# Unpacking 64-bit weights in a fused attention and feed-forward kernel: signs by GpSimd, half of a rescaling by ScalarE, one VectorE operation per block, scales from sums of squares

## The chip, the cores and the metric

The kernel runs on one core of one Trainium2 chip. The metric is the device time of one execution in microseconds (us), the median over runs. A profile of one execution is at hand: it lists every instruction with its engine, its start and its length, and what released it from a wait. PE is the matrix engine (TensorE), PEld its weight loads, DVE is VectorE, ACT is ScalarE, POOL is GpSimd, SPq is the queue on SyncE that issues the DMAs.

## The reference

Linear attention with exponential features, then a feed-forward layer with two weight matrices. Attention has 8 batches, 8 heads, 576 positions and head size 64; the feed-forward layer sees 4608 tokens of width 512 and has a hidden width of 2048.

```python
def phi(x):
    proj = np.einsum('bhsd,df->bhsf', x, w_phi)
    proj = proj - np.max(np.abs(proj), axis=-1, keepdims=True)
    return np.concatenate([np.exp(proj), np.exp(-proj)], axis=-1)
q_p, k_p = (phi(q), phi(k))
kv = np.einsum('bhsf,bhsd->bhfd', k_p, v)
z = np.sum(k_p, axis=2)
num = np.einsum('bhsf,bhfd->bhsd', q_p, kv)
den = np.einsum('bhsf,bhf->bhs', q_p, z)[..., None] + 1e-06
attn = num / den
...
h = x @ w_in          # x: attn as [4608, 512]
g = h * (1.0 / (1.0 + np.exp(-1.702 * h)))
return (g @ w_out).astype(np.float32)
```

The two weight matrices w_in [512, 2048] and w_out [2048, 512] arrive as 64-bit floats. The chip has no 64-bit arithmetic, so the kernel takes each number apart as two 32-bit words, `hi` (sign, exponent, upper bits of the mantissa) and `lo`.

## The kernel before, in words

Everything is recorded first: each operation on an engine goes into a list with its tiles and a group (`part`) with a due time. A planner (`Recorder.schedule`) then simulates the engines with estimated costs and writes out one fixed order per engine. Every engine, and the DMA queue on SyncE, later works through its own list strictly in that order. All planned instructions therefore carry line 346, the line that emits them, and are told apart by their tiles. Pools of tiles marked as ordered are handed out in the order of recording.

Attention runs batch by batch in four units of two heads; the first six units take a path with 32-bit products (`project_whole`: transposes with `ident`, products with `wb`, tiles `ab` for batch 0). Each unit ends with quotients `xf` (a reciprocal `rc`, a product), transposes of `xf` by PE, and two copies into the tile `x`, which the feed-forward layer reads. The last 64 positions of a batch go through `zt` (`attn_last`). The feed-forward layer (`moe_chunk`) works on 256 or 384 columns of `x` at a time: products with the first weights into `hb`, tanh (`th`), `g`, its split into two 16-bit parts `gh` and `gl`, products with the second weights into `ab`. The first two chunks run in two parts of the hidden width, so that they can start when half of the weights is there; the first part's result is kept (`kept`, written into an `x` tile).

The weights are 32 blocks of 128 x 512: block i is one of w_in for even i, of w_out for odd i, j = i // 2. `wbuf` holds one 32-bit block each in 33 slots. A block arrives as 512 KB of 64-bit numbers, either in a free stretch at the end of `wbuf` (12 blocks) or in one of three `x` tiles (20 blocks, two to a tile); the other users of the three `x` tiles are the batches' attention outputs. `load_weights` then unpacks it:

- POOL writes `y` = hi times 2^-112 into the block's slot, as a float (the 64-bit exponent moved into 32-bit range);
- ACT turns `lo` into its upper three bits, in place;
- DVE shifts y left by 3 and ORs the bits of lo in (`x<-wbuf,x`, or `wbuf<-wbuf`), then a second DVE operation takes the sign bit from hi and ORs it in, which gives the number in its slot (`wbuf<-x`, or `wbuf<-wbuf`);
- PE sums |number| over the partitions with the constant `pick`, in four products with 128 columns, on the 16 upper bits of the number without sign, which lie in the staging tile. So PE is the last reader of the staging tile.

After 16 blocks `weight_scales` makes a power of two from the largest sum, per matrix, with a short chain between DVE and PE; after it `split_weights` writes each block as two 16-bit parts (one ACT and one DVE operation per block, `wbuf<-wbuf,sw`). Only then can the feed-forward products of that half begin.

Of the kernel before, what the change touches and what calls it, by code (L numbers as in the profile page):

```python
# [8 lines left out]
F32 = mybir.dt.float32  # L9
F32R = mybir.dt.float32r  # L10
F16 = mybir.dt.float16
BF16 = mybir.dt.bfloat16
I32 = mybir.dt.int32
U32 = mybir.dt.uint32
# [335 lines left out]
def attn_moe_kernel(ctx, tc, q, k, v, w_phi, w_in, w_out, out):  # L350
# [76 lines left out]
    ones = cp.tile([16, P], F32, name="ones")  # L427
    nc.gpsimd.memset(ones, 1.0)

# [39 lines left out]

    NS = NJ // NH + 1  # L470
    pick = cp.tile([P, 2 * NS - 1], BF16, name="pick")
    nc.gpsimd.memset(pick, 0.0)
    nc.gpsimd.memset(pick[:, NS - 1 : NS], 1.0)

    def load_weights(j, wsum, first, last):
# [4 lines left out]
        for i, src in (  # L480
# [4 lines left out]
            if not WIDE:  # L485
# [3 lines left out]
                z = new("osb")  # L489
                R.scalar.activation(z, wbuf[:, i + 1], AF.Abs)  # L490
            else:
# [3 lines left out]
                else:  # L495
# [4 lines left out]
                lo, hi = r32[:, :, 0], r32[:, :, 1]  # L500
                y = wbuf[:, i + 1]
                R.gpsimd.tensor_scalar(y, hi.bitcast(F32), 2.0**-112, None, ALU.mult)
                z = lo
                R.scalar.activation(z, lo.bitcast(U32), AF.Copy, scale=0.9375 * 2.0**-29)
                R.vector.scalar_tensor_tensor(
                    z, y.bitcast(I32), 3, z, ALU.logical_shift_left, ALU.bitwise_or
                )
                R.vector.scalar_tensor_tensor(
                    dst.bitcast(I32), hi, -(2**31), z, ALU.bitwise_and, ALU.bitwise_or
                )  # L510
                z = raw.bitcast(BF16).rearrange("p (n w) -> p n w", w=4)[:, :, 1]

            r = NS - 1 if i % 2 else j % (NS - 1)
            for c in range(NCT):
                R.tensor.matmul(
                    wsum,
                    pick[:, NS - 1 - r : 2 * NS - 1 - r],
                    z[:, c * P : (c + 1) * P],
                    start=first and i % 2 + c == 0,
                    stop=last and i % 2 == 1 and c == NCT - 1,  # L520
                    skip_group_check=True,
                )
# [22 lines left out]
    def weight_scales(k, wsum):  # L545

        m = small(1, "sc")[0:NS]
        m2 = small(NS, "sc")[0:NS]
        R.vector.tensor_reduce(m, wsum, AX.X, ALU.max)
        pow2(m, m)  # L550
        R.vector.tensor_scalar(m2, ident[0:NS, 0:NS], m, None, ALU.mult)
        tp = psa()
        R.tensor.matmul(tp[:, 0:NS], ones[0:NS], m2, start=True, stop=True)
# [693 lines left out]
```

## Time and profile before

| | |
|---|---|
| median of 3 runs | 1096.73 us (1096.34 to 1098.07) |
| the profiled execution | 1097.82 us, span in the profile 1096.0 us, mean granted clock of PE 0.993 |
| PE busy | 1062.2 us (97%) |
| DVE busy | 857.8 us (78%) |
| ACT busy | 712.2 us (65%) |
| POOL busy | 242.4 us (22%) |

Busy time is that of whole instructions. The end of a matrix product is modelled in the profile, so a busy PE can hold some waiting. In rows of groups of instructions the columns are engine, operation, output and input tiles, shapes and types, count, then either least, median and largest length in ns with the first and last start in us, or busy time in us and mean length in ns followed by the engine's idle time in front of them and what ended it. In rows in order of time the first number is the start in us from the span's start, the second the length in us, and a bracket tells the idle time before it and its releaser.

### The profile page before, as it was taken

To read this page: it belongs to the slowest core of one execution; us is meant where nothing else is said; L and a number is where in the kernel's file an instruction comes from. 1 tells how busy PE (TensorE), PEld (TensorE's weight loads), DVE (VectorE), ACT (ScalarE), POOL (GpSimd) and SP (SyncE) were. 2 spreads that over 40 slices of the span, in tenths; PEclk is the share of its full clock that TensorE was granted. 3 is DMA by queue.
4 is the path that set the end of the run, shared out by engine and by line. 5 is a ranking of instruction groups with operands and counts; after the bars stand their busy time and mean duration, and the time that the engine had idled before them with its cause. 6 is when DMAs were issued, how large, how long until landed. Compare 5 with 4: busy or idle time off the path is not lost.

```text
span 1096.0 us, 22834 instructions
## 1 busy us (share of the span) xinstructions
PE 1062.2 (97%) x8915; PEld 733.2 (67%) x8915; DVE 857.8 (78%) x1775; ACT 712.2 (65%) x1483; POOL 242.4 (22%) x310
## 2 busy tenths in 40 slices
PE   5997999999999999999999999999999999999997
PEld 3664677778766666678766666677876666577653
DVE  5889988999989997897789987897779877422322
ACT  4576687977677776676777677685677666432423
POOL 6546201322121212221132221121123111100000
PEclk9998999999999999999999999999999999999999
DMA  8854233454243431442243433333223220000101
GB/s 273 277 185 130 76 92 84 79 107 98 61 93 92 96 89 36 81 107 57 32 102 88 109 88 55 64 97 60 49 68 68 39 59 10 11 30 1 30 1 29
DMA packets 174252, 87.80 MB, mean 80 GB/s; under 512 B 140224, under 2 KB 164928, under 8 KB 173888
## 3 DMA queue, kind: packets, MB, share of 16 engines
q1 hardware_dynamic: 174144, 86.34, 33.0%
q8 instruction: 70, 1.15, 0.5%
q14 instruction: 38, 0.31, 0.1%
HBM read 54.59 MB, written 9.44 MB: 58 GB/s over the span
## 4 chain that ended last, share of the span: by engine, by line
PE 78%; DVE 10%; ACT 4%; issue 3%; DMA 2%; POOL 1%; SPq 1%; ACTq 0%; DVEq 0%; POOLq 0%
PE ab L346 31%; PE hb L346 29%; PE at L346 19%; DMA xT<-xs 1%; DVE sm L346 1%; DVE gl L346 1%; ACT e L346 1%; DVE ks L346 1%; DVE g L346 1%; DVE t L346 1%; ACT eh L346 1%; SPq L346 1%; DVE el L346 1%; DVE elb L346 1%; DMA tl<-in_v_dram 1%
## 5 line engine op out<-in xcount | busy, mean ns | idle before, releaser
L346 PE MATMUL hb<-x,wbuf 128*128 128x192 f16 (+3 forms) x3264 | 474.9, 280 | 1.1 <-DVE g L346 1.1
L346 PE MATMUL ab<-wbuf,gh 128*128 128x512 f16 x1152 | 335.8, 380 | 0.8 <-ACT gh L346 0.6
L346 PEld LDWEIGHTS <-wbuf 128*128 128x128 f16 x3264 | 279.1, 98 | 78.0 <-issue 0.9
L346 ACT ACTIVATE th<-hb,usc 128x384 f32<-128x384 f32 (+1 forms) x208 | 116.4, 560 | 130.7 <-PE hb L346 125.0
L346 PE MATMUL ab<-wbuf,gl 128*128 128x512 f16 x576 | 192.2, 380 | 1.3 <-DVE gl L346 1.1
L346 DVE SCALAR_TENSOR_TENSOR g<-th,hb 128x384 f32<-128x384 f32 (+1 forms) x208 | 107.6, 517 | 89.8 <-ACT th L346 87.5
L346 PEld LDWEIGHTS <-gh 128*128 128x128 f16 x1152 | 107.3, 98 | 80.4 <-ACT gh L346 2.9
L346 ACT ACTIVATE gh<-g,al 128x384 f16<-128x384 f32 (+1 forms) x176 | 107.6, 611 | 62.7 <-DVE g L346 62.4
L346 DVE SCALAR_TENSOR_TENSOR gl<-g,al,gh 128x384 f16<-128x384 f32 (+1 forms) x176 | 110.9, 630 | 39.2 <-ACT gh L346 32.9
L346 POOL TENSOR_TENSOR xf<-nf,rc 128x512 f32<-128x512 f32 x28 | 32.8, 1171 | 459.4 <-DVE rc L346 395.1
L346 PE MATMUL at<-ph,xT 128*128 128x128 f16 x944 | 108.6, 221 | 0.4 <-ACT x L346 0.4
L346 ACT ACTIVATE e<-at 128x512 f32<-128x512 f32 x144 | 85.6, 602 | 30.3 <-PE at L346 28.5
L346 DVE TENSOR_REDUCE sm<-at 128x4 f32<-128x512 f32 x126 | 86.1, 683 | 21.3 <-PE at L346 21.1
L346 ACT ACTIVATE e<-t 128x512 f32<-128x512 f32 x144 | 89.9, 640 | 9.8 <-DVE t L346 8.6
L346 PEld LDWEIGHTS <-gl 128*128 128x128 f16 x576 | 55.1, 98 | 51.1 <-DVE gl L346 7.2
L346 DVE SCALAR_TENSOR_TENSOR t<-at,ks,sm 128x512 f32<-128x512 f32 x118 | 87.5, 744 | 1.0
L346 DVE TENSOR_TENSOR el<-e,eh 128x512 f16<-128x512 f32 (+1 forms) x106 | 74.7, 704 | 12.7 <-ACT eh L346 11.1
L346 PE MATMUL at<-vs,eh 128*128 128x132 f32 x208 | 80.2, 386 | 0.0
L346 DVE TENSOR_TENSOR elb<-e,eh 128x512 bf16<-128x512 f32 x104 | 74.8, 719 | 6.7 <-ACT eh L346 6.5
L346 PEld LDWEIGHTS <-xT 128*128 128x128 f16 x944 | 70.2, 98 | 14.3 <-issue 1.3
L346 PE MATMUL at<-kzs,eh 128*128 128x132 f32 x216 | 78.2, 375 | 0.0
L346 ACT ACTIVATE eh<-t 128x512 fp32r<-128x512 f32 x105 | 66.4, 648 | 0.3 <-DVE t L346 0.2
(205 smaller groups left out, 1896.4 us busy)
## 6 DMA issues: line engine op xcount, KB each, us to landing
vn<-in_v_dram SPq DMA_DIRECT2D x64, 128.0 KB, 2.9
kq<-in_k_dram SPq DMA_DIRECT2D x32, 256.0 KB, 3.2
kq<-in_q_dram SPq DMA_DIRECT2D x32, 256.0 KB, 3.0
tl<-in_v_dram SPq DMA_DIRECT2D x18, 384.0 KB, 3.2
x<-in_moe_w_in_dram SPq DMA_DIRECT2D x10, 512.0 KB, 5.3
x<-in_moe_w_out_dram SPq DMA_DIRECT2D x10, 512.0 KB, 4.8
out_dram<-osb SPq DMA_DIRECT2D x38, 128.0 KB, 2.4
out_dram<-osb SPq DMA_DIRECT2D x16, 256.0 KB, 2.5
```

The source lines that it names most:

```text
L346: f(*[g(a) for a in o.args], **{k: g(a) for k, a in o.kw.items()})
```

## The change

Four things change for each block. POOL no longer writes y for even blocks: ACT does (an activation with a scale), POOL still does for odd blocks. POOL gets a new operation for every block: it compares hi with zero and multiplies the outcome by -32768, written as a 16-bit integer into the upper half of each word of `lo` (so after ACT has written lo). DVE keeps one operation out of two: y shifted left by 3, OR lo, which now has the sign in it, in place in y. And PE squares the block: each 128 x 128 piece is multiplied with itself (its own columns as weights and as moving data, 16 upper bits of the finished number in its slot), added up per matrix in a 128 x 256 tile `wsq`, whose largest element is the largest sum of squares. `weight_scales` reduces the 128 partitions of wsq on DVE, transposes the result by PE, reduces again, halves the exponent with integer operations, and goes on as before. The constant `pick` and its two memsets go; a small constant `wone` comes.

```diff
--- before.py
+++ after.py
@@ -11,6 +11,7 @@
 F16 = mybir.dt.float16
 BF16 = mybir.dt.bfloat16
 I32 = mybir.dt.int32
+I16 = mybir.dt.int16
 U32 = mybir.dt.uint32
 I64 = mybir.dt.int64
 AF = mybir.ActivationFunctionType
@@ -424,8 +425,11 @@
     nc.vector.tensor_copy(ii[0:D], ident[0:D, 0:D])
     nc.vector.tensor_copy(ii[D:P], ident[D:P, D:P])
 
-    ones = cp.tile([16, P], F32, name="ones")
+    ones = cp.tile([2, P], F32, name="ones")
     nc.gpsimd.memset(ones, 1.0)
+    wone = cp.tile([2, 2], F32, name="wone")
+    nc.vector.tensor_scalar(wone[:, 0:1], ident[0:2, 0:1], 16.0, None, ALU.mult)
+    nc.vector.tensor_copy(wone[:, 1:2], ident[0:2, 1:2])
 
     wst = static("wst", [P, NF], F32)
     wb = static("wb", [P, 2 * NF], F32)
@@ -466,13 +470,7 @@
         )
         R.vector.tensor_scalar(dst, dst, 2.0**-50, None, ALU.max)
 
-
-    NS = NJ // NH + 1
-    pick = cp.tile([P, 2 * NS - 1], BF16, name="pick")
-    nc.gpsimd.memset(pick, 0.0)
-    nc.gpsimd.memset(pick[:, NS - 1 : NS], 1.0)
-
-    def load_weights(j, wsum, first, last):
+    def load_weights(j, wsq, first, last):
         js = slice(j * P, (j + 1) * P)
         stage = None
         if WIDE and (j % 4 > 1 or j >= NJ - 4):
@@ -486,8 +484,6 @@
                 if i % 2 == 0:
                     dst = dst.rearrange("p (c f) -> p c f", c=NCT)
                 R.sync.dma_start(dst, src)
-                z = new("osb")
-                R.scalar.activation(z, wbuf[:, i + 1], AF.Abs)
             else:
                 if stage is None:
                     s0 = NBLK - 7 + 2 * (i % 4)
@@ -498,24 +494,28 @@
                 R.sync.dma_start(rd, src)
                 r32 = raw.bitcast(I32).rearrange("p (n w) -> p n w", w=2)
                 lo, hi = r32[:, :, 0], r32[:, :, 1]
+
                 y = wbuf[:, i + 1]
-                R.gpsimd.tensor_scalar(y, hi.bitcast(F32), 2.0**-112, None, ALU.mult)
-                z = lo
-                R.scalar.activation(z, lo.bitcast(U32), AF.Copy, scale=0.9375 * 2.0**-29)
-                R.vector.scalar_tensor_tensor(
-                    z, y.bitcast(I32), 3, z, ALU.logical_shift_left, ALU.bitwise_or
+                R.scalar.activation(lo, lo.bitcast(U32), AF.Copy, scale=0.9375 * 2.0**-29)
+                if i % 2:
+                    R.gpsimd.tensor_scalar(y, hi.bitcast(F32), 2.0**-112, None, ALU.mult)
+                else:
+                    R.scalar.activation(y, hi.bitcast(F32), AF.Copy, scale=2.0**-112)
+                sign = raw.bitcast(I16).rearrange("p (n w) -> p n w", w=4)[:, :, 1]
+                R.gpsimd.tensor_scalar(
+                    sign, hi.bitcast(F32), 0.0, -(2.0**15), ALU.is_lt, ALU.mult
                 )
                 R.vector.scalar_tensor_tensor(
-                    dst.bitcast(I32), hi, -(2**31), z, ALU.bitwise_and, ALU.bitwise_or
+                    y.bitcast(I32), y.bitcast(I32), 3, lo, ALU.logical_shift_left, ALU.bitwise_or
                 )
-                z = raw.bitcast(BF16).rearrange("p (n w) -> p n w", w=4)[:, :, 1]
-
-            r = NS - 1 if i % 2 else j % (NS - 1)
+
+            z = wbuf[:, i + 1].bitcast(BF16).rearrange("p (n w) -> p n w", w=2)[:, :, 1]
             for c in range(NCT):
+                zc = z[:, c * P : (c + 1) * P]
                 R.tensor.matmul(
-                    wsum,
-                    pick[:, NS - 1 - r : 2 * NS - 1 - r],
-                    z[:, c * P : (c + 1) * P],
+                    wsq[:, i % 2],
+                    zc,
+                    zc,
                     start=first and i % 2 + c == 0,
                     stop=last and i % 2 == 1 and c == NCT - 1,
                     skip_group_check=True,
@@ -542,17 +542,25 @@
         R.tensor.matmul(tp[:, P : P + 1], ones[0:1], m2, start=True, stop=True)
         R.vector.tensor_copy(dst, tp[:, P : P + 1])
 
-    def weight_scales(k, wsum):
-
-        m = small(1, "sc")[0:NS]
-        m2 = small(NS, "sc")[0:NS]
-        R.vector.tensor_reduce(m, wsum, AX.X, ALU.max)
-        pow2(m, m)
-        R.vector.tensor_scalar(m2, ident[0:NS, 0:NS], m, None, ALU.mult)
+    def weight_scales(k, wsq):
+
+
+
+        m = small(2, "sc")
+        m1 = small(1, "sc")[0:2]
+        m2 = small(2, "sc")[0:2]
+        R.vector.tensor_reduce(m, wsq, AX.X, ALU.max)
         tp = psa()
-        R.tensor.matmul(tp[:, 0:NS], ones[0:NS], m2, start=True, stop=True)
-        R.vector.tensor_reduce(wg[:, k, 0:1], tp[:, 0 : NS - 1], AX.X, ALU.max)
-        R.vector.tensor_copy(wg[:, k, 1:2], tp[:, NS - 1 : NS])
+        R.tensor.transpose(tp[0:2, 0:P], m, ident)
+        R.vector.tensor_reduce(m1, tp[0:2, 0:P], AX.X, ALU.max)
+        R.vector.tensor_scalar(
+            m1.bitcast(I32), m1.bitcast(I32), 1, 0x7F800000,
+            ALU.logical_shift_right, ALU.bitwise_and,
+        )
+        R.vector.tensor_scalar(m1, m1, 2.0**64, 2.0**-50, ALU.mult, ALU.max)
+        R.vector.tensor_scalar(m2, wone, m1, None, ALU.mult)
+        R.tensor.matmul(tp[:, P : P + 2], ones[0:2], m2, start=True, stop=True)
+        R.vector.tensor_copy(wg[:, k], tp[:, P : P + 2])
         R.vector.reciprocal(sw[:, k], wg[:, k])
         R.vector.tensor_scalar(sw[:, k], sw[:, k], 2.0**14, None, ALU.mult)
         R.vector.tensor_mul(pg[:, k : k + 1], wg[:, k, 0:1], wg[:, k, 1:2])
@@ -1180,12 +1188,13 @@
     for part_ in range(NH):
         js = range(part_ * NJ // NH, (part_ + 1) * NJ // NH)
         v0, dv, v1 = WV[part_]
-        wsum = R.tile(ab if part_ else hb, whole=True)[0:NS, 0:P]
+        wsq = R.tile(ab if part_ else hb, whole=True)[:, 0 : 2 * P]
+        wsq = wsq.rearrange("p (t f) -> p t f", t=2)
         for i, j in enumerate(js):
             R.part(v0 + dv * i, v0 + dv * (i + 1))
-            load_weights(j, wsum, j == js[0], j == js[-1])
+            load_weights(j, wsq, j == js[0], j == js[-1])
         R.part(v1, v1)
-        weight_scales(part_, wsum)
+        weight_scales(part_, wsq)
         R.part(v1, v1 + 0.1, ("vector", "scalar"))
         for j in js:
             split_weights(j)
```

## Rows read from the trace of the kernel before

**Rows 1.** The page's slices: the span in 40 equal parts, PE's busy share of each in tenths, and the granted clock of PE in tenths of full speed.
```profile
PE   5997999999999999999999999999999999999997
PEclk9998999999999999999999999999999999999999
```

**Rows 2.** Busy time of each engine in four stretches of the span: start and end, length, busy us (and count) of PE, PEld, DVE, ACT and POOL, PE's mean granted clock, busy share of the DMA engines, GB/s.
```profile
12.00:97.00 85.00, 80.81 (x465) 54.76 (x466) 73.55 (x136) 56.80 (x114) 42.26 (x29) 1.00 0.72 232
97.00:113.00 16.00, 8.11 (x59) 6.01 (x58) 15.88 (x25) 10.55 (x20) 13.65 (x10) 0.60 0.65 186
113.00:140.00 27.00, 27.00 (x176) 18.18 (x175) 25.20 (x60) 19.15 (x39) 3.73 (x3) 0.98 0.16 47
...
140.00:1080.00 940.00, 934.54 (x8166) 648.49 (x8164) 737.87 (x1542) 618.91 (x1301) 175.66 (x242) 1.00 0.30 65
```

**Rows 3.** DVE's and ACT's operations on weights: least, median and largest length in ns, first and last start. The three DVE groups of int32 are the unpacking, the f16 group the splitting; the ACT groups of int32 are the treatment of lo.
```profile
L346 DVE SCALAR_TENSOR_TENSOR wbuf<-wbuf x24: 670/684/1121, 23.6 to 81.8; 128x512 int32<-128x512 int32 x24
L346 DVE SCALAR_TENSOR_TENSOR x<-wbuf,x x20: 646/685/1125, 34.6 to 126.4; 128x512 int32<-128x512 int32 x20
L346 DVE SCALAR_TENSOR_TENSOR wbuf<-x x20: 630/686/1151, 35.8 to 127.6; 128x512 int32<-128x512 int32 x20
L346 DVE SCALAR_TENSOR_TENSOR wbuf<-wbuf,sw x32: 732/751/1155, 88.7 to 172.0; 128x512 f16<-128x512 f32 x32
...
L346 ACT ACTIVATE wbuf<-wbuf x12: 661/698/744, 22.9 to 80.3; 128x512 int32<-128x512 uint32 x12
L346 ACT ACTIVATE x<-x x20: 641/675/743, 28.9 to 123.6; 128x512 int32<-128x512 uint32 x20
```

**Rows 4.** PE in order of time, the rows with a wait between 97 and 113 us, and the run of products that the last of them lets begin.
```profile
102.08 1.11 PE L346 MATMUL at<-ident,xf 128*128 128x128 f32 x4 [4.07 <-DVE xf L346]
...
105.76 0.40 PE L346 MATMUL at<-ii,zt 128*128 128x64 f16 x4 [2.01 <-ACT zt L346]
106.68 1.22 PE L346 MATMUL ab<-x,pick 128*9 128x128 bf16 x8 [0.53 <-DVE x L346]
...
111.08 0.62 PE L346 MATMUL ab<-x,pick 128*9 128x128 bf16 x4 [1.15 <-DVE x L346]
...
112.54 0.85 PE L346 MATMUL hb<-x,wbuf 128*128 128x256 f16 x3
```

**Rows 5.** All engines in order of time, 97 to 112 us: ACT's copy that the reciprocal needs, and what DVE and POOL do around it.
```profile
96.90 1.12 DVE L346 SCALAR_TENSOR_TENSOR wbuf<-x 128x512 int32<-128x512 int32 x1
...
98.41 0.36 ACT L346 COPY nf<-at 128x264 f32<-128x264 f32 x1
...
99.59 0.22 DVE L346 TENSOR_SCALAR rc<-nf,csx 128x8 f32<-128x8 f32 x1
...
101.35 0.68 DVE L346 TENSOR_TENSOR xf<-nf,rc 128x512 f32<-128x512 f32 x1
...
102.91 1.89 POOL L346 TENSOR_TENSOR xf<-nt,rc 64x256 f32<-64x256 f32 x2 [1.15 <-PE at L346]
...
105.50 1.72 DVE L346 SCALAR_TENSOR_TENSOR x<-wbuf,x 128x512 int32<-128x512 int32 x2
...
108.92 1.84 POOL L346 TENSOR_SCALAR wbuf<-x 128x512 f32<-128x512 f32 x1
109.30 1.12 DVE L346 SCALAR_TENSOR_TENSOR wbuf<-x 128x512 int32<-128x512 int32 x1
```

**Rows 6.** POOL's y between 12 and 120 us by form: busy time and mean ns, then idle time in front and what ended it.
```profile
L346 POOL TENSOR_SCALAR wbuf<-x 128x512 f32<-128x512 f32 x20 | 34.6, 1740 | 18.4 <-DMA x<-in_moe_w_in_dram 13.9 <-DMA x<-in_moe_w_out_dram 4.2
L346 POOL TENSOR_SCALAR wbuf<-wbuf 128x512 f32<-128x512 f32 x12 | 19.1, 1604 | 22.5 <-DMA wbuf<-in_moe_w_in_dram 15.5 <-DMA wbuf<-in_moe_w_out_dram 6.9
```

**Rows 7.** The same kind of groups for POOL's y over the whole span (least, median, largest length, first and last start), and a product of two tiles by POOL.
```profile
L346 POOL TENSOR_SCALAR wbuf<-x x20: 1507/1530/3489, 21.3 to 117.5; 128x512 f32<-128x512 f32 x20
L346 POOL TENSOR_SCALAR wbuf<-wbuf x12: 1519/1526/2009, 12.9 to 65.8; 128x512 f32<-128x512 f32 x12
...
L346 POOL TENSOR_TENSOR xo<-xf,xo 128x512 f16<-128x512 f32 x26 | 33.4, 1285 | 25.4 <-ACT xo L346 25.4
```

**Rows 8.** PE's sums with pick: a run of 16 products and the group that follows it, in order of time; weight loads of 9 columns, and of 128 columns in the feed-forward products.
```profile
86.71 2.01 PE L346 MATMUL ab<-wbuf,pick 128*9 128x128 bf16 x16
88.54 0.64 PE L346 MATMUL ab<-x,pick 128*9 128x128 bf16 x4
...
L346 PEld LDWEIGHTS <-pick x128: 83/105/109, 25.6 to 128.7; 128*9 128x9 bf16 x128
...
L346 PEld LDWEIGHTS <-wbuf x3264: 94/98/152, 90.2 to 1085.1; 128*128 128x128 f16 x192
```

**Rows 9.** The first half's scales in order of time on DVE: the first and the last operation of the chain, and the reduction of a transposed column and its PE product, from `allmax`, which has the same two steps as the new chain.
```profile
72.48 0.27 DVE L346 TENSOR_REDUCE sc<-hb 9x1 f32<-9x128 f32 x1
...
86.85 0.17 DVE L346 TENSOR_SCALAR sw<-sw 128x2 f32<-128x2 f32 x1
...
L346 PE MATMUL at<-ident,sc x2: 271/322/373, 7.1 to 57.9; 128*1 128x128 f32 x2
L346 DVE TENSOR_REDUCE sc<-at x2: 278/278/279, 7.6 to 58.2; 1x1 f32<-1x128 f32 x2
```

**Rows 10.** What comes after the second half's scales: the splits of all blocks (16 of the 32 before 126 us), and the first part's result being kept.
```profile
L346 ACT ACTIVATE wbuf<-wbuf,sw x32: 707/722/753, 87.3 to 170.6; 128x512 f16<-128x512 f32 x32
L346 ACT ACTIVATE x<-ab,osf x2: 687/690/693, 158.0 to 159.2; 128x512 f32<-128x512 f32 x2
```

## Prediction

> **What bounds the kernel now.** The page's slices come first. A slice is 27.4 us. PE is at nine tenths or more in all but the first, the fourth (82 to 110 us) and the last, and the granted clock is below full only in the fourth; so the long middle is a PE matter: between 140 and 1080 us PE is idle for 5.5 us of 940 [rows 1, 2]. The change touches only the loading of weights, whose unpacking runs from 23.6 to 127.6 us [rows 3]. What it can win is therefore PE time lost before that, and whatever is won or lost there is carried to the end, because behind 113 us PE has no gap to absorb it (27.00 busy of 27.00) [rows 2].
>
> Next, the stretches. From 12 to 97 us PE is busy 80.81 of 85.00 us, at full clock: 4.2 us of idle time in many small pieces. From 97 to 113 us it is busy 8.11 of 16.00 us, at a mean granted clock of 0.60, so part of it ran at the lower of the two levels, 1.2 GHz; its four longest pauses stand right there and sum to 7.76 us [rows 2, 4]. In the same 16 us DVE is busy 15.88 us and POOL 13.65 us [rows 2]. That is where the loss sits: the last unit of batch 0 ends there, the feed-forward layer cannot start before it, and DVE is full of weight work.
>
> The order of time shows what each pause waits for [rows 4, 5]. The first, 4.07 us, is for DVE's `xf`: ACT's copy nf ends at 98.77, the reciprocal's first step starts at 99.59, xf at 101.35, with weight work of DVE between. The second, 2.01 us, is for `zt`, which goes back to POOL's xf (1.89 us for two). The third and the fourth, 0.53 and 1.15 us, are PE's sums with pick waiting for DVE's first unpacking operation. The feed-forward run begins at 112.54 us, behind all of these in PE's fixed order.
>
> **The change part by part.**
>
> *DVE.* There are 64 unpacking operations (24 + 20 + 20) with medians of 684 to 686 ns [rows 3]; 32 go, 32 x 0.685 = 21.9 us. Most of it lies beside PE work and brings nothing: up to 97 us PE has a full list. In 97 to 113 us some eight of the 64 fall. The part on PE's path I take wait by wait. (a) The operation at 96.90 (1.12 us) is the second of its pair and goes; nf is ready at 98.77, the reciprocal starts at 99.59, so at most 0.8 us of the 4.07 us is DVE's backlog; I take 0.6. (b) The 2.01 us go over POOL and ACT: 0. (c) The 0.53 and 1.15 us stand behind DVE unpacking, such as 105.50 (1.72 us for two); these waits stay in kind, since PE then waits for the one operation left; I take half, 0.8. (d) The staging tile is free one DVE operation and one group of PE sums earlier, because PE now reads the slot and not the staging tile: 0.69 + 0.6 us in each turn. Two tiles take turns; with about three turns in the second half the blocks come some 3.9 us earlier, and one group or two fewer stand in front of the run at 112.54: a group is 0.62 to 0.64 us at its length [rows 4, 8]; I take 1.0. (e) PE ran part of the stretch at the lower clock; if the run begins 2.4 us earlier, that stretch is shorter by as much, at half rate: 0.9, counting that the first products then fall into it: I take 0.8. (f) Of the 4.2 us before 97 us I take 0.4. Sum of the gains: 0.6 + 0.8 + 1.0 + 0.8 + 0.4 = 3.6 us. Bounds: nothing at all, and 7.9 us (the whole idle time of the stretch) plus 2 us for the clock.
>
> *ACT.* 16 activations with a scale are added; the two groups for lo have medians of 675 and 698 ns, so 16 x 0.69 = 11.0 us [rows 3]. ACT is busy 56.80 of 85 and 10.55 of 16 us [rows 2]: it lies beside. One such activation in front of nf, a copy to x, or th costs the path up to 0.7 us; I take 0.3, bounds 0 and 1.4.
>
> *POOL.* 32 operations for y are 34.6 + 19.1 = 53.7 us, a mean of 1.68 and a median of 1.53 [rows 6, 7]. 16 go (26.9 us), 32 for the signs come. Their length S no row shows: two operations in one instruction, a comparison, a 16-bit result in steps of 8 bytes. The nearest row is y itself, same engine, same instruction with one arithmetic step, same reading pattern: 1.51 us at least. A product of two tiles with a 16-bit result takes 1.285 us [rows 7], so the 16-bit result alone is not dear. Upper bound: the pass over the data twice, 3.06 us. I take 1.9 us, nearer to y, with something for the second step. Then POOL has 26.9 + 32 x 1.9 = 87.7 us of weight work instead of 53.7. Between 12.9 and 119.1 us (106 us) it also has about 6 us of other work (59.64 busy in three stretches, less 53.7) [rows 2]: 94 of 106 us. It fits, because of POOL's idle time 40.9 us were waits for arriving weights [rows 6]. On the path it costs nothing as long as it fits; the point where it does not is (106 - 26.9 - 6) / 32 = 2.3 us. What is queued behind a sign on POOL: the xf and zt of a batch's last 64 columns, and in DVE's and PE's lists the shift-OR and the squares, with everything listed after them.
>
> *Latency of a block.* Before: y on POOL (1.53) beside lo on ACT, then two DVE operations (1.37). After, for an even block: lo (0.69), sign (1.9), one DVE operation (0.69); about the same, 3.3 against 2.9. An odd block has y in front of or behind its sign: up to 1.5 us more. Hidden by the other staging tile.
>
> *DVE and POOL at one memory.* While POOL's y ran at 108.92 for 1.84 us, a DVE operation on two tiles ran at 109.30 for 1.12 us: 0.3 and 0.4 us over their medians [rows 5, 3, 7]. So they slow each other, and both run. In 97 to 113 us POOL is busy 13.65 of 16 us already: little can be added, 0. Where POOL is less busy the DVE operations pay, beside PE work.
> The Trainium skill (SBUF — State Buffer, section Who interferes with whom) says otherwise: a DVE instruction with two inputs in this memory and a POOL instruction that reads it exclude each other, and the later one fully blocks until the first is done. The pair above ran together for 1.12 us, so the trace does not bear a full block out; what a full block would give is the third rival.
>
> *PE.* Four products of 128 columns per block stay four. 16 sums with pick took 88.54 - 86.71 = 1.83 us, 0.114 us each [rows 8]; the weight load, 9 columns before, is now 128 columns with a step of 4 bytes, the moving data's step goes from 8 to 4 bytes. Loads of 128 dense columns last 98 ns against 105 ns for pick [rows 8]. I take 0; bounds: -0.05 us each (a faster stream) and +0.08 us, or -6 to +10 us over 128 products, of which those before 97 us count in full.
>
> *Scales.* The chain of the first half runs from 72.48 to 87.02 us, 14.5 us, nearly all of it waiting in lists. The new one has one more PE product (0.32) and reduction (0.28) and a wider first reduction: about 0.7 us each half [rows 9]. The first run of feed-forward products begins 25 us after the first chain; after the second, whose blocks are split up to 170.6 us, the first part's result is put away only at 158.0 us [rows 10], so both are covered; without the cover 1.4 us. I take 0.
>
> **Sum.** -3.6 + 0.3 = -3.3 us. The profiled execution took 1097.82 us (span 1096.0 and 1.8 us around it), so the changed one would take 1094.5 us; the median of the runs is 1.1 us below the profiled execution, which gives 1093.4 us. Differences below 0.2%, 2.2 us, are about what a measurement of this kernel cannot tell from none.
>
> **The rivals.**
>
> *No gain (1096.7 us, within 2.2).* The 4.07 us are a chain of short steps between three engines and the order of the lists is made anew; DVE's freed time goes to other work while PE waits for the same steps plus a sign. For it: only 0.8 of those 4.07 us is backlog. Against it: DVE is busy 15.88 of 16 us there.
>
> *POOL becomes the bound (slower).* If S is over 2.3 us, signs come later than planned, and PE, in fixed order, waits at each group of squares. At S = 3.06 the weight work is 26.9 + 97.9 + 6 = 131 us in a window of 106, 25 us late. The last 12 groups or so stand among feed-forward products; if each holds PE for the longest wait there is now, 1.15 us, that is 14 us against 3.3 gained: 1107 us. For it: S is unseen, and POOL's one-step instruction is already slower than its product of two tiles. Against: POOL's 40.9 us of idle time.
>
> *DVE and POOL exclude each other (slower).* POOL's 94 us and DVE's two-input weight work (32 operations of 0.69 and 16 of 0.75 us, 34 us) would not fit side by side into 106 us: 22 us late, 12 to 14 us for PE by the same working, about 1107 us.
>
> *The front closes (1088 us).* The planner puts the feed-forward run right behind the copies to x, near 105 us, and the idle time of the stretch falls to a quarter: 6 us and the clock's 2.
>
> **How the numbers follow.** Forecast, a gain of 2.2 to 6 us: 0.46. Front closes, more than 6 us: 0.12. No change: 0.22. POOL the bound: 0.15. Exclusion: 0.02; PE's dearer weight loads or a worse order: 0.03. So faster 0.58, same 0.22, slower 0.20. The time is the forecast's, 1093.4 us, whose own range is 1090 to 1094.5. The range for 8 in 10 takes in the closing front down to 1087 us (leaving under 0.1) and the lighter half of the slower cases up to 1101 us (leaving 0.1).
>
> **What would show it.** Right: DVE has 32 unpacking operations; PE's idle time in the stretch before the first feed-forward run is 5 to 6 us instead of 7.9; that run begins 3 us earlier; POOL's signs take under 2.3 us; PE stays full behind it. Wrong: signs of 2.5 us or more with DVE waiting for POOL and PE for DVE in front of squares; groups of four squares longer than 0.6 us; pauses of PE behind 113 us, from an order that the planner makes otherwise.

## The result, and the profile after

The changed kernel takes 1105.88 us (median of 4 runs, 1105.8 to 1106.51) against 1097.4 us beside it: a ratio of 1.0072, interval 1.0058 to 1.0087. Forecast were 1093.4 us and a gain; it is slower by 0.72%, and 1105.88 lies above the range. The profiled execution took 1105.9 us, span 1104.1. One execution of a control further down (the kernel before with another price) took 2809 us; it is left out of that control's median and ratio.

In the changed kernel the line that emits all planned instructions is L347 (L349 where an edit adds two lines). The page's slices of the changed kernel: PE's and POOL's busy share and PE's granted clock in tenths.

```profile
PE   5896999999999999999999999999999999999997
...
POOL 5999901322112221221122211221123111100000
PEclk9997899999999999999999999999999999999999
```

The same four stretches as in [rows 2] (busy us of PE, PEld, DVE, ACT and POOL, each with its count, PE's granted clock, DMA share, GB/s):

```profile
12.00:97.00 85.00, 70.84 (x456) 50.07 (x456) 66.41 (x112) 63.40 (x126) 76.13 (x35) 1.00 0.70 226
97.00:113.00 16.00, 8.60 (x47) 5.03 (x48) 10.59 (x19) 11.58 (x23) 15.53 (x13) 0.53 0.58 165
113.00:140.00 27.00, 25.26 (x175) 17.99 (x174) 24.99 (x47) 17.24 (x35) 22.61 (x10) 0.90 0.38 114
140.00:1080.00 940.00, 932.70 (x8145) 645.89 (x8144) 739.33 (x1548) 619.15 (x1303) 174.74 (x242) 1.00 0.29 64
```

PE's idle time against [rows 2]: 12 to 97 us 14.2 (before 4.2), 97 to 113 us 7.4 (7.9), 113 to 140 us 1.7 (none), 140 to 1080 us 7.3 (5.5). That is 13.0 us more. PE's whole busy time fell from 1062.2 to 1057.2 us, 5.0 less. The two give 8.0 of the 8.1 us by which the span grew. So against the kernel before the added idle time lies mostly ahead of 97 us, while weights are unpacked, and not where the forecast looked (97 to 113 us). Not all of it is loss: the experiments' kernels that are faster than the kernel before also idle 9.5 to 10.5 us from 12 to 97 us. DVE got its relief (66.41 for 73.55, 10.59 for 15.88 us), and POOL is the fullest of DVE, ACT and POOL up to 113 us (76.13 of 85 and 15.53 of 16 us).

POOL's operations on weights between 10 and 150 us (busy us, mean ns, then idle time before them and what ended it); the first two groups are the signs, the others y, as in [rows 6]:

```profile
L347 POOL TENSOR_SCALAR x<-x 128x512 int16<-128x512 f32 x20 | 55.3, 2808 | 0.9 <-ACT x L347 0.7
L347 POOL TENSOR_SCALAR wbuf<-wbuf 128x512 int16<-128x512 f32 x12 | 32.4, 2748 | 13.1 <-ACT wbuf L347 13.1
L347 POOL TENSOR_SCALAR wbuf<-x 128x512 f32<-128x512 f32 x10 | 16.4, 1637 | 0.1
L347 POOL TENSOR_SCALAR wbuf<-wbuf 128x512 f32<-128x512 f32 x6 | 9.3, 1553 | 0.0
```

A sign takes 2.74 us on the mean, not 1.9. Its followers wait. DVE's waits, then PE's, from 10 to 150 us (total us, times, longest), first in the kernel before, then in the changed one:

```profile
DVE wbuf L346 <- POOL wbuf L346: 2.3, 1, 2.3
...
PE ab L346 <- DVE x L346: 1.7, 2, 1.2
...
PE hb L346 <- DVE x L346: 0.2, 1, 0.2
```

```profile
DVE wbuf L347 <- POOL x L347: 9.7, 11, 2.6
...
DVE wbuf L347 <- POOL wbuf L347: 3.5, 3, 1.5
...
PE ab L347 <- DVE wbuf L347: 4.8, 5, 1.3
PE ab L347 <- ACT t L347: 4.0, 4, 1.8
PE hb L347 <- DVE wbuf L347: 3.4, 3, 1.5
```

DVE waits 13.2 us for POOL where it waited 2.3 before; PE waits 8.2 us for unpacked blocks where it waited 1.9. DVE is less loaded and stands still more: its list, and PE's, place the shift-OR and the squares where the sign was expected, and everything listed after them waits too. PE in order of time shows it from 103 to 119 us, where batch 0 ends (compare [rows 4]):

```profile
103.86 1.12 PE L347 MATMUL at<-ident,xf 128*128 128x128 f32 x4 [1.81 <-DVE xf L347]
107.34 0.39 PE L347 MATMUL at<-ii,zt 128*128 128x64 f16 x4 [2.36 <-ACT zt L347]
...
110.70 0.39 PE L347 MATMUL at<-ii,zt 128*128 128x64 f16 x4 [2.46 <-POOL zt L347]
110.90 0.83 PE L347 MATMUL hb<-x,wbuf 128*128 128x256 f16 x3
...
114.80 0.61 PE L347 MATMUL ab<-wbuf 128*128 128x128 bf16 x4 [0.94 <-DVE wbuf L347]
...
118.69 1.47 PE L347 MATMUL hb<-x,wbuf 128*128 128x256 f16 x12
```

The pause for xf fell from 4.07 to 1.81 us, but another for POOL's zt came, and the feed-forward products, which begin at 112.54 us in [rows 4], begin at 110.90 us with three, after which PE stops again for a block; a long run of them begins only at 118.69 us. (In both kernels two single ones come before 95 us.)

What did the planner expect? Its price for such an operation of POOL is a line that the change doesn't touch, 100 + 3.4 n ns for n elements of a partition, so 1.84 us for 512. For y (1.53 us) that was 0.3 us too much, for a sign (2.74 us) it is 0.9 us too little.

### The profile page after: what moved, and what is told of

Read it like the earlier page. It is cut to its first block, busy times and chain, and to the rows that moved or that the text cites. A ratio compares the mean times of both kernels' runs of the same rounds, so it can differ in the third digit from the quotient of the medians.

```text
span 1104.1 us, 22841 instructions
## 1 busy us (share of the span) xinstructions
PE 1057.2 (96%) x8917; PEld 728.9 (66%) x8917; DVE 849.3 (77%) x1745; ACT 720.6 (65%) x1499; POOL 296.0 (27%) x324
## 4 chain that ended last, share of the span: by engine, by line
PE 76%; DVE 8%; POOL 8%; issue 2%; ACT 2%; DMA 2%; SPq 1%; ACTq 0%; DVEq 0%; POOLq 0%
PE ab L347 29%; PE hb L347 29%; PE at L347 17%; POOL x L347 4%; POOL wbuf L347 3%; DVE sm L347 1%; DVE t L347 1%; DVE ks L347 1%; DVE gl L347 1%; SPq L347 1%; DVE g L347 1%; DMA xT<-xs 1%; ACT e L347 1%; DVE el L347 1%; DVE elb L347 0%
## 5 line engine op out<-in xcount | busy, mean ns | idle before, releaser
L347 PE MATMUL hb<-x,wbuf 128*128 128x192 f16 (+3 forms) x3264 | 479.2, 280 | 2.1 <-DVE g L347 2.0
L347 PEld LDWEIGHTS <-wbuf 128*128 128x128 f16 (+1 forms) x3392 | 286.0, 98 | 89.3 <-DVE wbuf L347 11.1
L347 PE MATMUL ab<-wbuf,gh 128*128 128x512 f16 x1152 | 335.8, 380 | 0.0
L347 ACT ACTIVATE th<-hb,usc 128x384 f32<-128x384 f32 (+1 forms) x208 | 116.2, 559 | 136.3 <-PE hb L347 127.4
L347 PE MATMUL ab<-wbuf,gl 128*128 128x512 f16 x576 | 192.6, 380 | 1.1 <-DVE gl L347 0.9
L347 DVE SCALAR_TENSOR_TENSOR g<-th,hb 128x384 f32<-128x384 f32 (+1 forms) x208 | 107.3, 516 | 90.9 <-ACT th L347 88.6
L347 PEld LDWEIGHTS <-gh 128*128 128x128 f16 x1152 | 107.8, 98 | 79.2 <-ACT gh L347 1.9
L347 POOL TENSOR_TENSOR xf<-nf,rc 128x512 f32<-128x512 f32 x28 | 32.2, 1151 | 461.3 <-DVE rc L347 406.2
L347 ACT ACTIVATE gh<-g,al 128x384 f16<-128x384 f32 (+1 forms) x176 | 107.4, 610 | 62.5 <-DVE g L347 62.2
L347 DVE SCALAR_TENSOR_TENSOR gl<-g,al,gh 128x384 f16<-128x384 f32 (+1 forms) x176 | 111.5, 634 | 39.5 <-ACT gh L347 33.2
L347 PE MATMUL at<-ph,xT 128*128 128x128 f16 x944 | 110.4, 221 | 0.4 <-ACT x L347 0.4
L347 DVE TENSOR_REDUCE sm<-at 128x4 f32<-128x512 f32 x126 | 85.9, 682 | 21.5 <-PE at L347 21.3
L347 ACT ACTIVATE e<-at 128x512 f32<-128x512 f32 x144 | 85.4, 600 | 26.0 <-PE at L347 23.9
L347 ACT ACTIVATE e<-t 128x512 f32<-128x512 f32 x144 | 90.0, 639 | 14.1 <-DVE t L347 12.6
L347 PEld LDWEIGHTS <-gl 128*128 128x128 f16 x576 | 54.5, 98 | 52.6 <-DVE gl L347 8.9
L347 DVE SCALAR_TENSOR_TENSOR t<-at,ks,sm 128x512 f32<-128x512 f32 x118 | 87.5, 743 | 1.0
L347 DVE TENSOR_TENSOR el<-e,eh 128x512 f16<-128x512 f32 (+1 forms) x106 | 74.5, 703 | 16.8 <-ACT eh L347 14.1
L347 DVE TENSOR_TENSOR elb<-e,eh 128x512 bf16<-128x512 f32 x104 | 76.2, 732 | 6.9 <-ACT eh L347 6.8
L347 PEld LDWEIGHTS <-xT 128*128 128x128 f16 x944 | 70.9, 98 | 13.6 <-issue 0.5
L347 PE MATMUL at<-vs,eh 128*128 128x132 f32 x208 | 79.3, 382 | 0.0
L347 PE MATMUL at<-kzs,eh 128*128 128x132 f32 x216 | 77.3, 373 | 0.0
L347 ACT ACTIVATE eh<-t 128x512 fp32r<-128x512 f32 x105 | 66.3, 647 | 0.3 <-DVE t L347 0.2
```

What stands on the lines that cost most here:

```text
L347: f(*[g(a) for a in o.args], **{k: g(a) for k, a in o.kw.items()})
```

## Experiments

The theories, by the letters that the expectations use. A: POOL has too much work in all. B: the squares, or ACT's added operations, cost PE time. C: DVE and POOL exclude each other. D: the sign is longer than its price, so the fixed order puts DVE and PE in front of signs that aren't there. E: ACT is the bound once it has the y. F: any order made anew is better or worse by luck. G: DVE's relief is worth nothing, the gain is the squares'. Ratios are to the kernel before on the same chip, with 95% intervals.

### Which part costs

**Signs back on DVE**, all else as changed:

```diff
-                R.gpsimd.tensor_scalar(
-                    sign, hi.bitcast(F32), 0.0, -(2.0**15), ALU.is_lt, ALU.mult
-                )
+                R.vector.scalar_tensor_tensor(
+                    lo, y.bitcast(I32), 3, lo, ALU.logical_shift_left, ALU.bitwise_or
+                )
                 R.vector.scalar_tensor_tensor(
-                    y.bitcast(I32), y.bitcast(I32), 3, lo, ALU.logical_shift_left, ALU.bitwise_or
+                    y.bitcast(I32), hi, -(2**31), lo, ALU.bitwise_and, ALU.bitwise_or
                 )
```

> The changed kernel with one part undone: signs on DVE in a second operation, as before; y still half on ACT, squares by PE. Theory A (POOL is the bound, since a sign takes 2.75 us where 1.9 was assumed and 2.3 was the limit): POOL falls to 16 x 1.6 = 26 us of weight work, waits of PE on unpacking fall from 8.1 us to under 3, and the time returns below that of before, 1089 to 1096 us. Theory B (ACT's 16 added operations or the squares cost the time): stays near 1104 to 1106 us. Theory C (DVE and POOL exclude each other): also returns, but DVE's operations with two inputs, 0.98 us in the changed kernel against 0.68, shorten as well.

Measured: 1094.4 us, 0.9959 (0.9947 to 0.9971). The loss is gone, and 0.4% is won. PE in order of time around 105 us:

```profile
103.82 0.29 PE L347 MATMUL ab<-wbuf 128*128 128x128 bf16 x1 [2.52 <-DVE wbuf L347]
...
105.29 1.69 PE L347 MATMUL hb<-x,wbuf 128*128 128x256 f16 x7
```

PE still waits 6.9 us for unpacked blocks in all, where under 3 were expected, but the feed-forward run begins at 105.29 us. DVE's unpacking operations are back at a median of 0.69 us, so this run does not tell A, C and D apart.

**Every y on ACT**, signs on POOL: `R.scalar.activation(y, ..)` also for odd blocks.

> The changed kernel with every y on ACT: POOL keeps only the signs, 32 x 2.75 = 88 us plus 6 us of other work in a window of 106 us, so it fits; ACT gets 11 us more. Theory A (POOL's total is what counts): most of the loss goes, 1095 to 1100 us. Theory D (it is the planner, which counts a sign with 1.84 us, and so puts everything behind a sign too early): the signs are as mispriced as ever, and the time stays at 1103 us or more.

Measured: 1104.49 us, 1.0049 (1.0037 to 1.0061). With 25.7 us of y taken off POOL only 0.23% comes back, and DVE still waits 9.9 us for signs. So POOL's sum explains little of the loss.

**Squares alone**: the unpacking of before (y on POOL, two DVE operations), with squares and the new scales.

> The kernel before with only the weight scales changed: y for every block on POOL, both unpacking operations on DVE, squares of the finished numbers by PE instead of sums with pick. In the changed kernel six squares in a row took 0.36 us, 0.06 each, where sums took 0.114 to 0.126; so 128 x 0.06 = 7 us of PE work go, half of it or more where PE is full. Theory A and C: faster than before, 1091 to 1095 us. Theory B (the squares or the longer chain of the scales cost time): 1097 us or more.

Measured: 1094.77 us, 0.9965 (0.9953 to 0.9978), as much as with the signs on DVE (expected by A and C alike). Sixteen squares in order of time on PE, beside the 16 sums with pick of [rows 8]:

```profile
79.25 1.08 PE L347 MATMUL ab<-wbuf 128*128 128x128 bf16 x16
80.17 0.27 PE L347 MATMUL hb<-x,wbuf 128*128 128x256 f16 x1
```

80.17 - 79.25 = 0.92 us for 16, 0.058 us each, where sums took 0.114. Over 128 products that is 7.2 us of PE time.

### Late against the plan, or too much work

**The sign at its true price**: nothing but the planner's cost changes, so other orders of the same operations. Here a sign has 2.76 us and y 1.53.

```diff
         if meth == "tensor_scalar":
-            return 100 + 3.4 * n
+            if out.dtype == I16:
+                return 100 + 5.2 * n
+            return 100 + 2.8 * n
```

> The changed kernel with nothing changed but the planner's price for POOL: 2.76 us for a sign and 1.53 us for y, as measured, instead of 1.84 for both. Theory D (the wrong price made a bad order): back to 1098 us or less. Theory A (POOL's total of 113 us of weight work, 119 with the rest, does not fit into 106 us whatever the order): 1101 to 1106 us.

Measured: 1097.24 us, 0.9984 (0.9976 to 0.9993). DVE's waits for POOL in the same stretch, all of them:

```profile
DVE wbuf L349 <- POOL wbuf L349: 1.8, 1, 1.8
```

PE's waits for unpacked blocks, and the four stretches:

```profile
PE hb L349 <- DVE wbuf L349: 1.1, 2, 0.6
...
PE ab L349 <- DVE wbuf L349: 0.6, 1, 0.6
```

```profile
12.00:97.00 85.00, 74.58 (x460) 51.02 (x460) 65.81 (x116) 66.46 (x132) 77.10 (x34) 1.00 0.67 219
97.00:113.00 16.00, 11.24 (x77) 9.44 (x78) 14.96 (x26) 10.72 (x21) 14.17 (x9) 0.68 0.54 163
113.00:140.00 27.00, 26.27 (x183) 17.86 (x181) 23.32 (x40) 20.87 (x45) 22.15 (x17) 1.00 0.54 175
140.00:1080.00 940.00, 933.64 (x8148) 645.17 (x8148) 737.07 (x1550) 615.78 (x1293) 175.59 (x240) 1.00 0.28 63
```

DVE waits 1.8 us for POOL instead of 13.2; PE's waits for unpacked blocks are 1.7 instead of 8.2. POOL does the same work (113 us on weights), and the last unpacking operation starts even later, at 143.4 us (136.9 after, 127.6 before), yet 0.88% is back. With the same operations this is the comparison that shows where the changed kernel loses. PE's busy time is the same (1056.9 and 1057.2 us), and its idle time is smaller by 3.7 us from 12 to 97 us, 2.6 from 97 to 113, 1.0 from 113 to 140 and 0.9 from 140 to 1080 us, together 8.3 us of the 8.6 between the two spans (1104.1 and 1095.5 us).

**Every y on ACT, at the same prices.**

> Every y on ACT, as in the second run, and the planner's price of a sign 2.76 instead of 1.84 us. That run took 1104.5 us although POOL had only 85 us of signs. Theory D (the order is made from a price that is 0.9 us too low for each sign, so that DVE and PE stand in front of signs that are not there yet): DVE's waits for POOL, 9.9 us there, fall under 3, and the time falls by 6 us or more, to 1090 to 1098 us. Theory A (POOL's total): no change by the price, since the work is the same, 1102 to 1106 us. Theory E (ACT, with 32 more operations than before, holds PE up): stays over 1100 us.

Measured: 1098.38 us, 0.9997 (0.9988 to 1.0006). DVE's waits for POOL are 1.5 us, and the price again gives about 0.5% back, as D expected; taking the y off POOL gives nothing. A falls.

**A sign of one step**: the comparison alone, the price left at 1.84 us (its outcome is no sign bit: the weights have no sign).

```diff
-                R.gpsimd.tensor_scalar(
-                    sign, hi.bitcast(F32), 0.0, -(2.0**15), ALU.is_lt, ALU.mult
-                )
+                R.gpsimd.tensor_scalar(sign, hi.bitcast(F32), 0.0, None, ALU.is_lt)
```

> The changed kernel with the sign operation cut to one step: the comparison alone, written as before into 16 bits of each word, without the product with -32768. This leaves the sign out of the weights; the planner's price stays 1.84 us. It measures what the second step costs: if the length of a sign comes from the two steps, S falls from 2.75 to 1.5 to 1.9 us, if it comes from the 16-bit result in steps of 8 bytes, it stays above 2.4. With S under 1.9 theories A and D both give the forecast's side, 1090 to 1096 us; with S unchanged both give 1104 to 1106.

Measured: 1097.14 us, 0.9986 (0.9977 to 0.9995). Its signs (least, median, largest ns; first and last start):

```profile
L347 POOL TENSOR_SCALAR x<-x x20: 2237/2276/2602, 32.4 to 122.9; 128x512 int16<-128x512 f32 x20
```

2.28 us against 2.71 with both steps and y's 1.53; 0.43 us above the price, and DVE waits 4.2 us for POOL. Length and time both fall between the two cases that were expected. Since POOL's work and the gap to the price shrink together here, this run does not tell A from D.

**Signs priced at 2.30 us** (100 + 4.3 n) **and at 3.68 us** (100 + 7.0 n), y at 1.53, operations as changed.

> The changed kernel with a sign priced at 2.30 us, half way between the 1.84 of the changed kernel (1105.9 us) and the 2.76 of the fourth run (1097.2 us), and y at 1.53. Theory D: in between, 1099 to 1104 us, with DVE's waits for POOL between 13.2 and 1.8 us. Theory F (luck of an order): no relation to the two neighbours; DVE's waits may be anything.

> The changed kernel with a sign priced at 3.68 us, 0.9 us above its length, y at 1.53. Theory D: a price too high makes nobody wait for POOL; the planner only puts the weights later than they need be. DVE's waits for POOL stay under 2 us as at 2.76, and the time is that of the run at 2.76 (1097.2 us) or up to 4 us more, since POOL would be planned to work until about 165 us. Theory F (luck): no relation.

Measured: 1101.12 us, 1.0023 (1.0014 to 1.0032), with 10.4 us of DVE's waits for POOL, as D expected; and 1115.66 us, 1.0154 (1.014 to 1.0167), with none. Here D's expectation of at most some 1101 us failed: nobody waits for POOL, but too high a price is worse than too low a one. The last unpacking operation begins at 161.5 us, and from 140 to 1080 us PE is idle for 18.4 us (6.4 at the right price), in part because it waits for blocks. PE's waits in that stretch:

```profile
PE ab L349 <- DVE wbuf L349: 8.7, 3, 3.9
PE hb L349 <- DVE g L349: 3.1, 6, 0.7
```

### Controls, and what DVE's relief is worth

**The kernel before with y priced at 1.53 us** and **the signs back on DVE with that price**.

> The kernel before with one number of the planner changed: POOL's y priced at 1.53 us, as measured, instead of 1.84. A control: how far does any new order move the time? Theory D: the old price was too high by 0.3 us, which costs little (an operation that is there early holds nobody), within 2 us of 1097 to 1099. Theory F (any change of order moves the time by several us, and the 8 us of the fourth run were such luck): 3 us or more off, either way.

> The first run (signs on DVE, half of y on ACT, squares; 1094.4 us) with POOL's y priced at 1.53 us, as measured. Theory D: the old price of 1.84 was on the harmless side, so the time stays within 2 us, 1092.5 to 1096.5 us.

Measured: 1100.15 us, 1.001 (0.9995 to 1.0026), and 1095.34 us, 0.9967 (0.9956 to 0.9978). The price of y explains none of what the sign's price gives back.

**No sign at all** (the weights have no sign): DVE's second operation is saved and POOL pays nothing.

```diff
-                R.gpsimd.tensor_scalar(
-                    sign, hi.bitcast(F32), 0.0, -(2.0**15), ALU.is_lt, ALU.mult
-                )
```

> The changed kernel without any sign operation: half of y on ACT, one DVE operation per block, squares by PE, and the sign left out of the weights. So DVE is relieved of 32 operations at no price on POOL: this is the whole gain the prediction put on that relief. By the prediction's sum (3.6 us) against the first run, which has the two DVE operations, 1094.4 us: 1089 to 1092 us. Theory G (DVE's relief is worth nothing on PE's path, and what e1 and e3 gained over the kernel before is the cheaper squares alone): 1093 to 1096 us.

Measured: 1094.35 us, 0.9963 (0.995 to 0.9975): no better than with two DVE operations (0.9959, 0.9965). The relief, had for free, is worth nothing that can be measured. The orders of these kernels lie within 0.1% of one another, so a gain under about 1 us cannot be excluded; one of 3.6 us would show, unless this one order were unlucky by as much. PE's waits for blocks, then PE in order of time:

```profile
PE ab L347 <- DVE wbuf L347: 4.7, 2, 2.4
...
PE hb L347 <- DVE wbuf L347: 1.8, 3, 1.4
```

```profile
99.05 0.63 PE L347 MATMUL at<-ident,xf 128*128 128x128 f32 x4 [2.13 <-DVE xf L347]
102.05 1.04 PE L347 MATMUL ab<-wbuf 128*128 128x128 bf16 x8 [2.37 <-DVE wbuf L347]
...
105.59 0.29 PE L347 MATMUL ab<-wbuf 128*128 128x128 bf16 x1 [2.30 <-DVE wbuf L347]
...
106.21 4.89 PE L347 MATMUL hb<-x,wbuf 128*128 128x256 f16 x22
```

With 32 DVE operations fewer, PE still pauses three times for over 2 us in front of the run.

**Sums with pick on the finished numbers** in the kernel before: moving data in steps of 4 bytes, not 8 (the numbers have their sign there, so the sums, and the scales, come out otherwise).

```diff
-                z = raw.bitcast(BF16).rearrange("p (n w) -> p n w", w=4)[:, :, 1]
+                z = wbuf[:, i + 1].bitcast(BF16).rearrange("p (n w) -> p n w", w=2)[:, :, 1]
```

> The kernel before with one edit: the sums with pick read the 16 upper bits of the finished number in its slot (a step of 4 bytes) instead of the staging tile (a step of 8 bytes). The weight load stays at 9 columns. The sums are then of signed numbers, so the scales are wrong; nothing else differs. If the step of the moving data made the sums slow (0.114 to 0.126 us against 0.06 for a square), they fall to about 0.06 us each and the time to that of the third run, 1094 to 1096 us. If the narrow weight load made them slow (105 ns each), they stay at 0.11 or more and the time at 1097 to 1099 us.

Measured: 1102.29 us, 1.0028 (1.0017 to 1.0039). Loads of pick and products (least, median, largest ns), and a run of 20 with the group behind it in order of time:

```profile
L346 PEld LDWEIGHTS <-pick x128: 83/86/129, 28.1 to 128.0; 128*9 128x9 bf16 x128
...
L346 PE MATMUL hb<-wbuf,pick x64: 218/218/225, 28.1 to 74.0; 128*9 128x128 bf16 x64
```

```profile
88.00 1.30 PE L346 MATMUL ab<-wbuf,pick 128*9 128x128 bf16 x20
89.23 0.28 PE L346 MATMUL hb<-x,wbuf 128*128 128x256 f16 x1
```

A product lasts 218 ns (294 before, the median of the 48 from `x`) and the load of pick 86 ns ([rows 8]: 105); 20 take 1.23 us (89.23 - 88.00), 0.062 us each, where a sum took 0.114 before [rows 8]. So the step was what made the sums slow, not the squares what made them fast. But the time got worse, against the expected 1094 to 1096 us, from an order that differs: PE waits 6.3 us for ACT's t and 4.5 us for unpacked blocks. Why this order is worse was not settled. It shows that an order made anew can move the time by 0.3% (F, in part), so a single kernel's 0.35% would not prove a gain; four orders with squares and without a sign on POOL's list (0.9959, 0.9963, 0.9965, 0.9967) agree, and that is what the gain rests on. That it comes from the cheaper products is argued, not shown: this run has them too, with the staging tile released as early, and is slower. The four also share the new scales.

## Why the prediction was wrong, step by step

**The sum.** The step that failed first is POOL's term: the signs were put at 0 on PE's path, since POOL's work fits, and cost some 12 us. DVE's relief was put at -3.6 us and is worth nothing measurable. Squares and scales were put at 0 and bring about 4 us. ACT's 0.3 us is too small to be told. 12 - 4 = 8 us, which is the measured loss (0.72%, 7.9 us).

**The sign's length.** Taken 1.9 us, measured 2.71 (median; bounds 1.51 to 3.06 held it). The reasoning "nearer to y, with something for the second step" failed on both halves: one step alone takes 2.28 us, 0.75 over y (the comparison and the 16-bit result together; not told apart), and the second step adds 0.43 us.

**The point at which it matters.** The prediction named the right rival ("signs come later than planned, and PE, in fixed order, waits at each group of squares") and gave it 0.15 by a wrong measure: POOL's capacity, limit 2.3 us. That rival's 1107 us lies 1 us from the measured time by luck: it was worked out from signs of 3.06 us and from blocks that come 25 us late. What decides most is the sign's length against the planner's price of 1.84 us, which it did not look up. With the same operations and POOL's same load, the right price took the time from 1.0072 to 0.9984, about 9.7 us; unloading POOL of every y took 2.5 us without the price and nothing with it. By capacity, the kernel with the right price, whose blocks come latest, should have been the slowest of these. It is not: in its order PE idles about 8 us less, though the blocks come later. The price gap is not the whole law: at nearly the same gap (0.41 and 0.43 us) the two kernels stand at 1.0023 and 0.9986, the second with 15 us less of signs on POOL (73.4 us for 88.2) or a luckier order.

What the signs cost in all is 1.0072 against 0.9963 without them, about 12 us: 9.7 of it the price, the other 2.3 us open.

**DVE's relief, (a) to (f), -3.6 us.** Measured: nothing (0.9963 against 0.9959 and 0.9965). The step that failed is (c) and what followed from it: halving the unpacking was to halve PE's waits for it. With the relief free, they are 6.5 us where they were 1.9, and 5.8 to 6.9 us with two DVE operations: cheaper squares may bring PE there earlier, where it waits for blocks instead, but that is not shown, and with the right price, one DVE operation and squares, the waits are 1.7 us. (a) was right in kind, the 4.07 us wait for xf is down to 1.81 in the changed kernel, but it falls as well where DVE has no relief (3.0 us with the squares alone, 0.3 with the signs on DVE), so the order made anew suffices for it. (b), no gain, held; but a new wait of 2.46 us for POOL's zt came, which the prediction had named as queued behind a sign and given no price. The rival "no gain" gave this reason: the freed time goes to other work while PE waits for the same steps.

**Squares.** Taken 0, bounds -6 to +10 us. They free 7.2 us of PE time, just outside the bound; the four kernels with squares and no sign on POOL are 3.6 to 4.5 us faster than the kernel before. Cheaper products, new scales and the earlier release of the staging tile (1.0 us in (d)) are all in these 3.6 to 4.5 us and were not measured apart. The prediction saw the shorter step of the moving data and judged the run by the weight load; sixteen squares, each with a load of 128 columns, took 0.92 us, so the loads (98 ns in [rows 8]) overlap, and the step was the term.

**ACT's activations and the scales.** ACT with 16 more (signs on DVE) is at 0.9959 against 0.9965 without: the 0.3 us can't be told from nothing. The new scales run in all the fast kernels; alone they were not measured. B falls, and so does E as the cause: with every y on ACT at the right price the time is that of the kernel before.

**Exclusion.** The price at 0 per pair was too low in one place. In the changed kernel DVE's shift-ORs from the `x` tiles have a median of 978 ns, and in order of time the slow ones start right behind a sign, with POOL's next operation:

```profile
32.49 2.74 POOL L347 TENSOR_SCALAR x<-x 128x512 int16<-128x512 f32 x1
...
32.73 1.01 DVE L347 SCALAR_TENSOR_TENSOR wbuf<-wbuf 128x512 int32<-128x512 int32 x1 [1.37 <-POOL wbuf L347]
...
35.02 1.56 POOL L347 TENSOR_SCALAR wbuf<-x 128x512 f32<-128x512 f32 x1
...
35.26 1.00 DVE L347 SCALAR_TENSOR_TENSOR wbuf<-wbuf,x 128x512 int32<-128x512 int32 x1 [1.52 <-POOL x L347]
```

With the right price, in the same order of time, one that did not wait takes its usual 0.68 us beside two signs:

```profile
37.40 5.21 POOL L349 TENSOR_SCALAR x<-x 128x512 int16<-128x512 f32 x2
...
37.93 0.68 DVE L349 SCALAR_TENSOR_TENSOR wbuf<-wbuf,x 128x512 int32<-128x512 int32 x1
```

The start decides most. In the changed kernel 16 of the 32 shift-ORs start 0.20 to 0.25 us after an operation of POOL, and 15 of these take 0.98 to 1.02 us; all 13 that start 0.37 us or more after one still running take 0.68 us. With the right price 20 of the 22 that start 0.54 us or more after one take 0.67 to 0.69 us, two take 1.12 and 1.16. The rule of the Trainium skill (SBUF — State Buffer, section Who interferes with whom), an exclusive lock under which the later of such a pair would have to wait until the other is done, is not what these rows show: 0.3 us at some starts, nothing at others. C falls as the cause: all slow shift-ORs together cost DVE 4.6 us in the changed kernel (15 of 32) and 3.2 us with the right price (8 of 32), a difference of 1.4 us beside the 9.7 us that the price gives back.

**The clock.** It was to gain 0.8 us; the granted clock from 97 to 113 us was 0.53 instead of 0.60 (0.65 to 0.68 in the four faster kernels and with the right price). Behind 113 us the forecast was right that nothing is absorbed: PE idled 1.7 us more in 113 to 140 us and 1.8 us more in the middle, and the rest of the loss arrived at the end whole.

**The better versions.** Squares and new scales with two DVE operations, y all on POOL (1094.77 us) or half on ACT (1094.4 us), take 0.35 to 0.4% less than the kernel before, and 1% less than the changed one. That is the part of the change to keep.

## What to carry to other kernels

Where a planner writes fixed orders, read its price of a new operation and hold it against the operation's measured length: a sign 0.9 us over its price cost some 9.7 us here, with the same work on every engine, and a price 0.9 us too high some 19 us (1.0154 against 0.9984). Relieving DVE of 32 operations gave nothing here, since PE's pauses remained. An order made anew moved the time by up to 0.3% by itself, so a small gain wants more than one order. For a new instruction of POOL time each arithmetic step and the output's form, and don't take its price from a one-step neighbour.

## What the runs showed of the hardware

- POOL, 128 x 512 32-bit inputs in steps of 8 bytes: one step with a 32-bit result 1.53 us, a comparison with a 16-bit result in steps of 8 bytes 2.28 us, comparison and product 2.71 us.
- PE, products of 128 columns of 16-bit moving data: in steps of 8 bytes 0.114 us each in a run of 16, in steps of 4 bytes 0.062 us in a run of 20 with 9 columns of weights and 0.058 us in a run of 16 with 128.
- DVE beside POOL: a two-input operation of 0.68 us takes 0.97 to 1.02 us in 18 of 19 starts 0.20 to 0.25 us behind the start of an operation of POOL, and 0.67 to 0.69 us in 33 of 35 starts 0.37 us or more behind it, while it still runs (the changed kernel and the same at the right price, taken together); why the other three differ stays open.
